# Naming the coming branch and its case ahead of each conditional weight split

## The chip, the cores and the metric

The kernel runs on one core of a Trainium2 chip. The metric is the device time of one execution in microseconds. The engines have short names in the profile: PE is TensorE (PEld its weight loads), DVE is VectorE, ACT is ScalarE, POOL is GpSimd, SP is SyncE, whose queue issues most of the DMAs. Each has a sequencer of its own, which takes the engine's instructions in order, handles registers, waits and branches by itself, and hands the rest to the engine.

## The reference

A retention layer without softmax (8 batches, 8 heads, 576 positions, head size 64), then two expert layers on its 4608 rows of 512. Each row goes to one of 8 experts, the one with the largest logit, and through that expert's two matrices with a relu between.

```python
scores = scale * np.matmul(q, k.transpose(0, 1, 3, 2))
ret = scores * Dmat[None, :, :, :]
x = np.matmul(ret, v)                 # then as rows [4608, 512]
...
expert_idx = np.argmax(logits, axis=1)
for e in range(E):
    mask = expert_idx == e
    h = np.maximum(x[mask] @ w1[e], 0.0)
    out[mask] = gate_w[mask, None] * (h @ w2[e])
```

The second expert layer does the same with its own gates and weights, and an output gate for each expert.

## The kernel before

Attention runs over 36 units of 128 tokens and scatters its rows by expert into a table in device memory, from which the first expert layer reads slots of 128 rows, all of one expert. It scatters its results into a second table for the second layer, which works alike and scatters to the output. Which expert a slot belongs to is known only at run time.

A product is made to about full precision from two parts of each operand: a high part rounded for fast TensorE passes and a low part, the difference. For the weights, `split_all` makes the parts from the raw buffers raw1 and raw2: ScalarE and VectorE copy the high parts (w1h, w2h, lines 298 and 299), VectorE and GpSimd subtract for the low ones (w1l, w2l, line 300). This is needed only at an expert's first slot, once for w1 and once for w2. So `switch(s, w)` (line 811) puts it into a two-way branch on ScalarE, VectorE and GpSimd: case 1 holds the split, case 0 holds nothing. `tc.Switch` gives each case a body that begins with a hint instruction naming the code behind the branch and ends with a jump there. The case is bit s of a mask that these engines hold in registers. After the branch SyncE refills the raw buffer for the next expert, if there is one to fetch.

The program gives every engine's order by hand. `period(t, n)` (line 1021) is one slot: TensorE makes slot t's first product (`first`, line 831), ScalarE and VectorE take its halves through the relu (`relu`, line 847), the next slot's rows are transposed and split (`trans_x`: xth on ScalarE, xtl on VectorE), then comes `switch(t + 1, 1)`, then the second product of slot t - 1 (`second`, line 865), the routing for the second layer (layer 1 only: route2a, route2b, chunk_logits with the copy lsb, and x1t), then `switch(t, 2)`, and `trans_h(t)` (line 855), in which ScalarE makes hth and VectorE htl for the second product of slot t. So each slot passes two branches, one for w1 of the next slot and one for w2 of its own. Layer 2 has `store` in place of the routing (oix on VectorE, line 889). The layers' last periods stand inside a further branch on the number of slots (line 1065).

In the profile the hint of a body has line 814, and the register and branch instructions of the dispatch have line 1259, the launch line.

Of the kernel before, what the change touches and what calls it, by code (L numbers as in the profile page):

```python
# [35 lines left out]

# columns of the constant table
C_ID = 0
# [23 lines left out]
def unit_table():  # L62
    """Units of 128 tokens: (batches, chunk); chunk 4 holds the tails of two batches."""
    u = []
    for bp in range(B // 2):
        for c in range(4):
            u.append(((2 * bp,), c))
            u.append(((2 * bp + 1,), c))
        u.append(((2 * bp, 2 * bp + 1), 4))
    return u  # L70
# [3 lines left out]
def retention_moe_moe(ctx, tc, qh, kth, kh, vh, embT, tau, w1, w2, wg, v1, v2, const, out):  # L74
# [51 lines left out]
    def inv_norm(pool, ss, n, tag, eng):  # L126
        """1 / (sqrt(ss) + 1e-6) by Newton steps on the reciprocal square root: tile and operations."""
        V = nc.vector
# [27 lines left out]
    def slot_tables(tab, cum_last, cum_part, psum):  # L156
        """From the counts, with slots along partitions: each slot's first row, which of its rows are
        its own, its expert's first slot, the next expert to fetch; and whether the first 256 rows of
        expert 0 were there by cum_part. TensorE's first step, the operations in order, and how many come
        before its second one (the last three serve the stores only); psum() gives a bank."""  # L160
        val, inv, ti, tf = tab
# [95 lines left out]
    def scatter_rows(key, table, rows, ix, n):  # L257
        """Rows to table[ix]; those past n are left out. No two scatters of a key share a row."""
        i = nc.gpsimd.indirect_dma_start(  # L259
            out=table,  # L260
            out_offset=bass.IndirectOffsetOnAxis(ap=ix, axis=0),
            in_=rows,
            in_offset=None,
            bounds_check=n - 1,
            oob_is_err=False,
        ).ins
        tc.declare_no_dep(i, group=key, reason="each row of the table is written by one scatter")
        tc.add_to_no_dep_group(key, i)
# [3 lines left out]
    def zero_heads(bk, i):  # L272
        """A third of the rows that a slot may read past those an expert has."""
        for r in ([e * NT for e in range(E)] + [P])[3 * i : 3 * i + 3]:
# [4 lines left out]
    def load_first(bk):  # L279
        """The first two tiles of expert 0's rows, ahead of the counts."""  # L280
        for i in range(2):
            nc.sync.dma_start(xs[i], bk[i * P : i * P + P, :])

    def split(i, r1, r2, w):
        """hi/lo parts of chunk i of w1 (w=1) or w2 (w=2): on which engine each half goes."""
        if w == 1:
# [7 lines left out]
    def split_ops(w, r1, r2):  # L294
        """The operations that split all of w1 or w2: hi(i) on ScalarE, sub(engine, i, columns) for lo, and
        for VectorE hi_v(i)."""
        ch = [split(i, r1, r2, w) for i in range(4)]
# [7 lines left out]
    def split_lists(w, r1, r2):  # L305
        """The same, shared out: for ScalarE, VectorE and GpSimd."""
        hi, hi_v, sub = split_ops(w, r1, r2)
# [10 lines left out]
    def load_raw(r1, r2, wa, wb, e, i=None):  # L318
        """Expert e's weights, whole or chunk i of 8 only."""
        for k in range(4):  # L320
# [7 lines left out]

    # ------------------------------------------------------------ attention
    ch = ExitStack()  # L330
    ch1 = ch.enter_context(tc.tile_pool(name="ch1", bufs=1, side="right"))
    ch2 = ch.enter_context(tc.tile_pool(name="ch2", bufs=2, side="right"))
    with ExitStack() as actx:
# [41 lines left out]

        # the tensor engine warms up while the first loads are under way
        nc.vector.memset(warm, 0.0)
# [107 lines left out]
        def cross(u):  # L485
            """The queries on the state before their unit."""
            bs, c = units[u]
# [117 lines left out]
        def pump(n):  # L605
            """Emit up to n queued small operations; one of TensorE opens a call or waits for the next."""
            first = True
# [155 lines left out]

    # ------------------------------------------------------------ experts
    mp = ctx.enter_context(tc.tile_pool(name="mp", bufs=1, reuse_waits="tile"))
# [10 lines left out]
    for t in orow:  # L776
        nc.gpsimd.memset(t[:, DM:ROW], 0.0)

    engs = {ET.DVE: nc.vector, ET.Pool: nc.gpsimd, ET.Activation: nc.scalar}
    everyone = {ET.PE: nc.tensor, ET.SP: nc.sync, **engs}  # L780
# [4 lines left out]
    def layer(which):  # L785
        """One expert layer's steps, by slot of 128 rows."""
        L = SimpleNamespace()
# [3 lines left out]
        ps_h, ps_o, rt, pk, sreg = {}, {}, {}, {}, {}  # L791
        L.state = (ps_h, ps_o, rt, pk, sreg)
        out_rows = (lambda s: orow[s % 4]) if g else (lambda s: yrow[s % 3])
# [17 lines left out]
        def switch(s, w):  # L811
            """At an expert's first slot: its weights from the raw buffer to their parts, the next one's there."""
            m, b = (L.mask[0], s) if s < NB else (L.mask[1], s - NB)
            for case in tc.Switch({e: (r >> b) & 1 for e, r in m.items()}, 2):  # L814
                if case == 1:
                    split_all(w, L.r1, L.r2)
            if w == 1:
                fetched(s)
            refill(w, *sreg[s])

        def fetched(s):
# [76 lines left out]
        def chunk_logits(s, copy=nc.scalar.copy):  # L898
            """Both gates' logits by chunk of 128 features, each chunk in its own 32 columns of the array."""
            rt[s] = pl = bank("M", f"pl{s}")  # L900
# [14 lines left out]
        def route2a(s):  # L915
            """Expert and place of each row of the second table: operations, the one-hots first."""
            V = nc.vector
# [56 lines left out]
        def redo():  # L974
            """Slots 0 and 1 again, now with the rows and the weights that the counts ask for."""
            masks()
# [15 lines left out]
        def begin(fail, late):  # L992
            """With the tables there: the loads that hang on them, slots 0 and 1 again if their rows were
            others, and the rest of these up to slot 0's second product."""
            for s in range(2, 5):
# [25 lines left out]
        def period(t, n):  # L1021
            """Slot t's first product, the one before's second, and what goes with them."""
            first(t)
# [3 lines left out]
            if t + 1 < n:  # L1027
                trans_x(t + 1)
                switch(t + 1, 1)
            second(t - 1, range(4))  # L1030
            if g and t >= 3:
# [50 lines left out]

    # attention's last tile goes to its expert while expert 0's first rows are at work
    psum = lambda: bank("C", "tabs")
# [30 lines left out]
    def turnover(n):  # L1115
        """The first layer's last slots to their experts while the second layer starts on expert 0."""
        for d in L2.state:
# [96 lines left out]
def _layout(inputs):  # L1214
# [4 lines left out]
    def units(a):  # L1219
        # [B, H, S, D] -> [units, 128 tokens, H, D]  # L1220
        a = a.transpose(0, 2, 1, 3)
# [41 lines left out]
```

## Time and profile before

| | us |
|---|---|
| median of 3 runs | 1527.78 |
| the three runs | 1527.77, 1527.78, 1530.72 |
| span of the profiled execution | 1519.3 |
| TensorE busy in that span | 1301.2 |
| VectorE busy | 634.8 |
| ScalarE busy | 420.0 |
| GpSimd busy | 369.6 |

The span runs from the first to the last instruction of the profiled execution; the time of a run also holds what lies before and behind it. Busy time counts operations on data alone. Registers, branches, waits and hints are the sequencer's and are not in it, and the timeline doesn't list them: their places are found by asking for their source line in a narrow stretch, which gives starts to a tenth of a microsecond.

### The profile page before, as it was taken

What the parts mean: (1) busy time and instruction counts of PE and PEld (TensorE: products, weight loads), DVE (VectorE), ACT (ScalarE), POOL (GpSimd) and SP (SyncE); (2) the same over time, 40 slices, a digit from 0 to 9 for tenths busy, and PEclk for the clock granted to TensorE, in tenths of its full rate; (3) what the DMA queues carried; (4) which work ended last, traced back from release to release, by engine and by line L of the source; (5) the groups of instructions that cost most, each with busy time, mean ns of one, the idle gap of its engine ahead of it and who ended that gap; (6) DMA issues with size and microseconds to landing.
All of it is one profiled execution on the core that took longest, in us unless ns stands there. A gap on an engine that the chain in (4) does not pass through costs nothing. (4 is left out here: it accounts for less than half of the span.)

```text
span 1519.3 us, 25914 instructions
## 1 busy us (share of the span) xinstructions
PE 1301.2 (86%) x7620; PEld 1051.6 (69%) x7620; DVE 634.8 (42%) x1589; ACT 420.0 (28%) x871; POOL 369.6 (24%) x431
## 2 busy tenths in 40 slices
PE   8899986888788887979788886898998789898988
PEld 7899975666566665757666674686776667676776
DVE  4566751443534444442544436124233442533331
ACT  2344431222222232322312222122232231322322
POOL 3477640220302121210212203003021221312121
PEclk9999998989899898989999998899998899999999
DMA  9999936233222214141231101413232433243110
GB/s 260 270 312 289 275 116 188 92 123 114 92 90 93 93 34 147 33 146 53 92 107 39 38 26 48 139 54 137 63 106 93 146 106 104 94 148 107 48 43 31
DMA packets 94255, 174.27 MB, mean 115 GB/s; under 512 B 8796, under 2 KB 36828, under 8 KB 92768
## 3 DMA queue, kind: packets, MB, share of 16 engines
q1 hardware_dynamic: 82144, 132.15, 28.8%
q0 software_dynamic: 9120, 28.91, 5.1%
q14 instruction: 1415, 11.59, 2.7%
q8 instruction: 72, 1.18, 0.3%
q10 hardware_dynamic: 1504, 0.43, 0.2%
HBM read 391.94 MB, written 35.36 MB: 281 GB/s over the span
## 5 line engine op out<-in xcount | busy, mean ns | idle before, releaser
L873 PE MATMUL po<-w2h,htl 128*128 128x512 f32 x624 | 270.8, 434 | 104.4 <-DVE htl L863 103.9
L873 PE MATMUL po<-w2h,hth 128*128 128x512 f32 x624 | 273.8, 439 | 23.3 <-ACT hth L862 21.7
L873 PE MATMUL po<-w2l,hth 128*128 128x512 f32 x624 | 262.4, 420 | 5.4 <-DVE w2l L300 5.4
L863 DVE TENSOR_TENSOR htl<-pt,hth 128x512 fp32r<-128x512 f32 x156 | 100.4, 684 | 381.5 <-issue 201.8
L873 PEld LDWEIGHTS po<-w2h,htl 128*128 128x128 f32 x624 | 129.1, 207 | 154.9 <-DVE htl L863 127.2
L838 PE MATMUL ph<-w1h,xth 128*128 128x512 f32 x624 | 206.4, 413 | 14.8 <-issue 10.9
L838 PE MATMUL ph<-w1l,xth 128*128 128x512 f32 x624 | 200.6, 403 | 9.3 <-DVE w1l L300 8.7
L838 PE MATMUL ph<-w1h,xtl 128*128 128x512 f32 x624 | 196.7, 397 | 0.0
L873 PEld LDWEIGHTS po<-w2h,hth 128*128 128x128 f32 x624 | 129.1, 207 | 56.1 <-ACT hth L862 23.6
L873 PEld LDWEIGHTS po<-w2l,hth 128*128 128x128 f32 x624 | 128.8, 206 | 33.0 <-DVE w2l L300 8.0
L862 ACT CAST hth<-pt 128x512 fp32r<-128x512 f32 x156 | 83.8, 588 | 244.6 <-issue 227.4
L838 PEld LDWEIGHTS ph<-w1l,xth 128*128 128x128 f32 x624 | 118.4, 193 | 45.0 <-DVE w1l L300 20.3
L259 POOL DMA_INDIRECT bk<-orow,bix x39 | 38.8, 996 | 444.5 <-DVE orow L967 288.1
L838 PEld LDWEIGHTS ph<-w1h,xtl 128*128 128x128 f32 x624 | 119.7, 192 | 26.9
L838 PEld LDWEIGHTS ph<-w1h,xth 128*128 128x128 f32 x624 | 113.9, 194 | 35.2 <-issue 16.1
L259 POOL DMA_INDIRECT out_dram<-yrow,oix x39 | 38.3, 982 | 389.8 <-ACTq L814 223.7
L300 POOL TENSOR_TENSOR w1l<-raw,w1h 128x1024 fp32r<-128x1024 f32 (+1 forms) x28 | 76.4, 2749 | 157.2 <-DVE w1h L299 157.2
L454 PE MATMUL sc<-qt,kt 128*128 128x128 f32 x576 | 83.6, 288 | 8.5 <-DMA kt<-in_kth_dram 7.6
L300 DVE TENSOR_TENSOR w1l<-raw,w1h 128x1024 fp32r<-128x1024 f32 (+1 forms) x42 | 87.4, 2133 | 0.0
L883 ACT ACTIVATE yrow<-po,xg 128x512 f32<-128x512 f32 x37 | 25.4, 688 | 211.9 <-PE po L873 169.6
L861 PE MATMUL pt<-ident,hs 128*128 128x128 f32 x624 | 83.2, 277 | 0.0
L300 DVE TENSOR_TENSOR w2l<-raw,w2h 128x1024 fp32r<-128x1024 f32 (+1 forms) x42 | 82.1, 2008 | 1.8 <-ACT w2h L298 1.8
(205 smaller groups left out, 1590.0 us busy)
## 6 DMA issues: line engine op xcount, KB each, us to landing
raw<-in_w_dram SPq DMA_DIRECT2D x77, 2048.0 KB
raw<-in_v_dram SPq DMA_DIRECT2D x77, 2048.0 KB
xg<-bk SPq DMA_DIRECT2D x74, 264.0 KB
qt<-in_qh_dram SPq DMA_DIRECT2D x36, 256.0 KB
vr<-in_vh_dram SPq DMA_DIRECT2D x36, 256.0 KB
kr<-in_kh_dram SPq DMA_DIRECT2D x36, 256.0 KB
kt<-in_kth_dram SPq DMA_DIRECT2D x70, 128.0 KB
bk<-z SPq DMA_DIRECT2D x18, 264.0 KB
```

What stands on the lines that cost most here:

```text
L259: i = nc.gpsimd.indirect_dma_start(out=table, out_offset=bass.IndirectOffsetOnAxis(ap=ix, axis=0), in_=rows, in_offset=None, bounds_check= ...
L300: sub = lambda eng, i, c=slice(0, FF): lambda: eng.tensor_sub(ch[i][1][:, c], ch[i][2][:, c], ch[i][0][:, c])
L454: nc.tensor.matmul(ps[:, j * P : j * P + P], k_t[:, hp, h, :], q_t[:, hp, :], start=(j == 0), stop=True, skip_group_check=True,)
L838: nc.tensor.matmul(ps_h[s][i], st[:, k, :], wt[:, i * 512 : i * 512 + 512], start=(k == 0 and wt is w1h[k] and st is xh), stop=(k == 3 or ...
L861: nc.tensor.transpose(ps[:, f, :], hsb[s % 2][:, o : o + P], ident)
L862: nc.scalar.copy(hth[s % 2][:, h, :], ps)
L863: nc.vector.tensor_sub(htl[s % 2][:, h, :], ps, hth[s % 2][:, h, :])
L873: nc.tensor.matmul(po, st[:, f, :], wt[:, b, :], start=(f == 0 and st is hh and wt is w2h[a]), stop=(f == 7 and st is hl),)
L883: nc.scalar.activation(o[:, 0:DM], ps_o.pop(s), AF.Copy, scale=x[:, DM : DM + 1])
```

## The change

`period` gets two calls of a new function `ahead(s, w)`. It asks for a hint instruction that names the branch of `switch(s, w)` and its case, worked out from the same mask bit, on the three engines that take the branch. The hint for w1 of the next slot stands at the start of a slot, ahead of its first product (from t = 3 on); the hint for w2 of the slot itself stands right behind the w1 branch and its refill. `switch` takes the label of the hint, so that hint and branch belong together. The bodies, the splits, the refills and all other operations are as before. (The diff also drops comments and docstrings, left out here.)

```diff
+        L.hints = {}
+        L.state = (ps_h, ps_o, rt, pk, sreg, L.hints)
...
         def switch(s, w):
-            m, b = (L.mask[0], s) if s < NB else (L.mask[1], s - NB)
-            for case in tc.Switch({e: (r >> b) & 1 for e, r in m.items()}, 2):
+            label = L.hints.pop((s, w), None)
+            for case in tc.Switch(at_first(s), 2, hint=label):
                 if case == 1:
                     split_all(w, L.r1, L.r2)
             if w == 1:
                 fetched(s)
             refill(w, *sreg[s])
+
+        def at_first(s):
+            m, b = (L.mask[0], s) if s < NB else (L.mask[1], s - NB)
+            return {e: (r >> b) & 1 for e, r in m.items()}
+
+        def ahead(s, w):
+            L.hints[s, w] = tc.switch_hint(at_first(s), 2, label=f"sw{which}_{s}_{w}_{next(uid)}")
...
         def period(t, n):
+            if t + 1 < n and t >= 3:
+                ahead(t + 1, 1)
             first(t)
             relu(t)
             if g:
                 trans_g(t - 2)
             if t + 1 < n:
                 trans_x(t + 1)
                 switch(t + 1, 1)
+                if t < n - 1:
+                    ahead(t, 2)
             second(t - 1, range(4))
```

## Rows read from the trace of the kernel before

**Rows 1.** In the page, its part on busy time: busy us, share of the span and instructions of each engine.
```profile
PE 1301.2 (86%) x7620; PEld 1051.6 (69%) x7620; DVE 634.8 (42%) x1589; ACT 420.0 (28%) x871; POOL 369.6 (24%) x431
```

**Rows 2.** The waits of the whole span. Columns: who waited at which line, for whom; us in total, times, longest us. "issue" is time in which the engine waited for nothing that the profile shows.
```profile
DVE htl L863 <- issue: 201.8, 33, 8.4
...
PE po L873 <- DVE htl L863: 103.9, 44, 5.5
...
DVE w2h L299 <- issue: 29.5, 9, 4.0
...
DVE w1h L299 <- issue: 28.4, 14, 3.3
...
PE pl L913 <- ACT lsb L910: 19.6, 13, 3.1
...
DVE w2h L299 <- PE px L827: 18.1, 5, 3.7
```

**Rows 3.** In the page, its part on DMA queues: the queue that carries instructions. Columns: packets, MB, share of 16 engines' time.
```profile
q14 instruction: 1415, 11.59, 2.7%
```

**Rows 4.** The instructions of line 814 over the whole span, those of the sequencers (DVEq is VectorE's). Columns: count, duration in ns (least, median, most), first and last start in us. The hint instruction stands first in each body of a branch.
```profile
L814 POOLq BRANCH_PREFETCH_HINT  x150: 31/38/43, 225.4 to 1498.9; - x150
L814 ACTq BRANCH_PREFETCH_HINT  x150: 31/31/36, 230.5 to 1505.0; - x150
L814 DVEq BRANCH_PREFETCH_HINT  x150: 39/44/45, 231.3 to 1505.6; - x150
```

**Rows 5.** The timeline of VectorE in a quiet slot of layer 1, 533 to 544 us. Columns: start us, us, engine, line, operation, tiles, shapes, count, and in brackets the idle time before it and what ended it.
```profile
533.73 0.17 DVE L962 SCALAR_TENSOR_TENSOR t<-pk,oh 128x8 f32<-128x8 f32 x1 [3.61 <-PE pt L861]
...
539.71 1.29 DVE L863 TENSOR_TENSOR htl<-pt,hth 128x512 fp32r<-128x512 f32 x2 [5.54 <-issue]
...
542.56 0.15 DVE L945 TENSOR_SCALAR W<-W 128x1 f32<-128x1 f32 x1 [0.16 <-ACT t L937]
542.63 0.68 DVE L853 TENSOR_SCALAR hs<-ph 128x512 f32<-128x512 f32 x1
```

**Rows 6.** The branch instructions of VectorE's sequencer in that slot (line 1259, where the program's own branches are recorded) and the hints that open the bodies (line 814), each answer for a narrow stretch. Columns as in rows 4.
```profile
L1259 DVEq COMPARE_BRANCH  x2: 52/64/75, 529.6 to 530.3; - x2
...
L1259 DVEq COMPARE_BRANCH  x1: 48/48/48, 534.4 to 534.4; - x1
...
L814 DVEq BRANCH_PREFETCH_HINT  x1: 44/44/44, 536.1 to 536.1; - x1
...
L1259 DVEq COMPARE_BRANCH  x1: 75/75/75, 536.3 to 536.3; - x1
...
L1259 DVEq MOVE  x2: 36/36/36, 543.6 to 543.7; - x2
...
L1259 DVEq COMPARE_BRANCH  x2: 52/64/75, 544.0 to 544.7; - x2
...
L814 DVEq BRANCH_PREFETCH_HINT  x1: 44/44/44, 544.5 to 544.5; - x1
```

**Rows 7.** The timeline of ScalarE in the same slot. Columns as in rows 5.
```profile
543.00 0.57 ACT L828 CAST xth<-px 128x512 fp32r<-128x512 f32 x1
```

**Rows 8.** The timeline of TensorE, in that slot and behind a split of w1 in layer 1. Columns as in rows 5.
```profile
543.96 0.17 PE L951 MATMUL pk<-oh,slb 128*128 128x8 bf16 x1 [0.73 <-DVE x1t L896]
...
653.05 0.79 PE L873 MATMUL po<-w2h,htl 128*128 128x512 f32 x1 [4.61 <-DVE htl L863]
```

**Rows 9.** The timeline of VectorE around a split of w1 in layer 1, 633 to 654 us. Columns as in rows 5.
```profile
633.01 0.15 DVE L945 TENSOR_SCALAR W<-W 128x1 f32<-128x1 f32 x1 [0.16 <-ACT t L937]
...
652.31 1.29 DVE L863 TENSOR_TENSOR htl<-pt,hth 128x512 fp32r<-128x512 f32 x2 [7.47 <-issue]
```

**Rows 10.** The last branch of VectorE ahead of that split and the hint in the split's body, and the same for a split of w2 in layer 1 (line 1259 and line 814 in narrow stretches). Columns as in rows 4.
```profile
L1259 DVEq COMPARE_BRANCH  x1: 48/48/48, 634.5 to 634.5; - x1
...
L814 DVEq BRANCH_PREFETCH_HINT  x1: 44/44/44, 637.5 to 637.5; - x1
...
L1259 DVEq COMPARE_BRANCH  x1: 52/52/52, 661.4 to 661.4; - x1
...
L814 DVEq BRANCH_PREFETCH_HINT  x1: 44/44/44, 664.2 to 664.2; - x1
```

**Rows 11.** The timeline of VectorE ahead of that split of w2: its first operation behind the way out of the branch before. Columns as in rows 5.
```profile
660.72 0.17 DVE L962 SCALAR_TENSOR_TENSOR t<-pk,oh 128x8 f32<-128x8 f32 x1 [3.61 <-issue]
```

**Rows 12.** The timeline of VectorE in layer 2, a quiet slot and the beginning of one with a split of w1. Columns as in rows 5.
```profile
1096.86 1.29 DVE L863 TENSOR_TENSOR htl<-pt,hth 128x512 fp32r<-128x512 f32 x2 [6.79 <-ACT hs L849]
...
1109.65 1.29 DVE L863 TENSOR_TENSOR htl<-pt,hth 128x512 fp32r<-128x512 f32 x2 [6.20 <-issue]
```

**Rows 13.** VectorE's branches and hints of those two (line 1259 and line 814 in narrow stretches). Columns as in rows 4.
```profile
L1259 DVEq COMPARE_BRANCH  x1: 48/48/48, 1097.6 to 1097.6; - x1
...
L814 DVEq BRANCH_PREFETCH_HINT  x1: 39/39/39, 1099.5 to 1099.5; - x1
...
L1259 DVEq COMPARE_BRANCH  x1: 48/48/48, 1110.7 to 1110.7; - x1
...
L814 DVEq BRANCH_PREFETCH_HINT  x1: 44/44/44, 1113.5 to 1113.5; - x1
```

**Rows 14.** ScalarE's sequencer in a split of w1 in layer 2: the hint in the body (line 814) and its first instruction behind the branch (line 883), in a narrow stretch. Columns as in rows 4.
```profile
L814 ACTq BRANCH_PREFETCH_HINT  x1: 31/31/31, 1025.2 to 1025.2; - x1
...
L883 ACTq EVENT_SEMAPHORE  x1: 38/38/38, 1027.3 to 1027.3; - x1
```

More of the change, by code (lines that the diff above doesn't have):

```diff
@@ L1 @@
+import itertools
 from contextlib import ExitStack
@@ L777, in retention_moe_moe @@
         nc.gpsimd.memset(t[:, DM:ROW], 0.0)
+    uid = itertools.count()
     engs = {ET.DVE: nc.vector, ET.Pool: nc.gpsimd, ET.Activation: nc.scalar}
@@ L791, in layer @@
         ps_h, ps_o, rt, pk, sreg = {}, {}, {}, {}, {}
-        L.state = (ps_h, ps_o, rt, pk, sreg)
+        L.hints = {}
+        L.state = (ps_h, ps_o, rt, pk, sreg, L.hints)
         out_rows = (lambda s: orow[s % 4]) if g else (lambda s: yrow[s % 3])
```

## The prediction

> **What bounds the kernel now.** I read first the busy shares, then the waits, then one quiet slot and one slot of each kind of split on VectorE, with the branch instructions of those slots.
>
> TensorE is busy 86% of the span, VectorE 42% [rows 1]. By shares alone TensorE is the bound. But the waits say that TensorE's largest idle time, 103.9 us in 44 pieces, is for htl, which VectorE writes, and that VectorE in its turn stood 201.8 us before htl with nothing to wait for that the profile shows [rows 2]. Such "issue" time is what a branch costs: the engine's next instructions are not there yet. Each of the three engines passes 150 of these branches [rows 4], and the queue that carries instructions moved 11.59 MB in 1415 packets [rows 3], some 8.2 KB each and some three packets for each of the 450 passes.
>
> In a quiet slot of layer 1 this can be timed. VectorE enters the empty body at 536.1, branches out some 0.2 us later, and its next operation, htl, starts at 539.71: the way out takes 3.4 us. The way in, from the branch at 534.4, takes 1.7 us; at the other branch, from 544.0 to 544.5, it takes 0.5 us [rows 5, 6]. Between the ways, VectorE works without a break (the one gap it has in 539.7 to 544.5 is 0.16 us). The slot therefore lasts as long as VectorE's loop, 14.4 us (the same branch stood at 529.6), and TensorE waits 0.73 us in it for x1t [rows 8]. So the resource that counts is VectorE's sequencer, and the four block fetches of a slot are more than half of it.
>
> Why does the way in differ? After a way out, the block behind the present one is on its way by itself: 533.7 (first operation after the way out) to 536.1 is 2.4 us, and by 544.5 it had long arrived, so that only 0.5 us was left [rows 5, 6]. The empty body lies in that next block, the split body one block further. A split body is thus entered late whatever came before: 634.5 to 637.5 is 3.0 us, 661.4 to 664.2 is 2.8 us [rows 10], and in layer 2 1110.7 to 1113.5 is 2.8 us [rows 13].
>
> **The change part by part.** It takes nothing away. It adds, per slot and engine, two groups of about six sequencer instructions. The branch itself is prepared by such a group, from its first MOVE at 543.6 to the branch at 544.0, and the hint instruction takes 0.04 us [rows 4, 6]: I price a hint at 0.45 us of VectorE's sequencer. ScalarE and GpSimd get the same.
>
> It can help only the way in, since the way out keeps the hint that already stands first in each body, and 3.4 us is what it costs with that hint. For an empty body it can help little: at 0.5 us there is nothing left, and where the way in takes 1.7 us the new hint stands right behind the way out, and names the block that is already coming.
>
> What is left are the splits: 14 of w1 and 14 of w2 (VectorE stood 28.4 us before the first operation of the one, 29.5 and 18.1 us before the other [rows 2]), half of them in each layer. The gain is not the 3 us of a way in but the lead that VectorE's program gives, because the hint is queued on the same engine behind its other work:
> - w1, layer 1. The hint can stand behind L945, at 633.01 [rows 9]; at 0.45 us it is out at 633.5. With the 3.0 us that the fetch took when it was asked for at the branch, the body is there at 636.5 instead of 637.5: 1.0 us, seven times, 7 us. The split, the way out behind it and htl at 652.31 [rows 9] move up by as much, and with htl TensorE, which waited 4.61 us for it [rows 8].
> - w1, layer 2. VectorE comes out at 1109.65, so the hint is out at 1110.2, and 3.0 us later is 1113.2 instead of 1113.5 [rows 12, 13]: 0.3 us, seven times, 2 us.
> - w2, both layers. VectorE comes out at 660.7 [rows 11], has only the few small operations of route2b, and branches at 661.4. The hint is out at 661.1 and the body there at 664.0 instead of 664.2: 0.2 us, fourteen times, 3 us. "Half a slot ahead" in the program is 0.3 us ahead here, as VectorE spent that half slot in the branch before.
>
> Together 12 us. Both ends: nothing, if the hint's block queues behind the one that comes by itself; and 28.4 + 29.5 + 18.1 = 76 us [rows 2] if every wait ahead of a split went.
>
> The costs. In a quiet slot of layer 1, the first group stands between L945 and the relu at 542.63. Relu and x1t start up to 0.45 us later, but the sequencer had to wait for xth in any case: the first MOVE of the branch is at 543.6, and ScalarE's xth ended at 543.57 [rows 6, 7]. So what counts is how far ScalarE's own group delays xth. The trace doesn't show it: 0 to 0.45 us, of which I take 0.2. Layer 1 has 150 / 2 / 2, some 37 such slots; without the seven of each split and the seven whose ways out are slowed by the refill (7.47 us before htl at 652.31 [rows 9]), 16 quiet ones are left: 3 us (0 to 7). The second group stands behind the way out, where the block of the next branch takes its 2.4 us regardless: nothing; if that cover went, 0.45 us a slot. In layer 2 the way in at 1097.6 ended at 1099.5, 2.6 us after htl's start at 1096.86 [rows 12, 13], so that both groups lie beside a fetch: nothing. On ScalarE the second group is ahead of lsb, for which TensorE waited 19.6 us in 13 pieces [rows 2]; some seven of them have ScalarE come straight out of a branch, at 0.4 us each: 3 us. GpSimd waits for others nearly always; its split operations come behind VectorE's first. Nothing moves on SyncE and no DMA of data is added.
>
> Sum: 12 - 3 - 3 = 6 us gained. The profiled execution has a span of 1519.3 us and the median is 1527.78, so 8.5 us lie around the span and don't change. **Forecast: 1522 us.** Its own range, from no gain with the costs to twice the gain, is 1510 to 1534.
>
> [...] In quiet slots a way in of 0.5 us shows that the next block had been fetched unasked [rows 6]. [...]
>
> **The rivals.**
> - A hinted block comes faster than one that is asked for at the branch. For: ScalarE entered a split body at 1025.2 with its hint, and had an instruction from behind the branch at 1027.3, 2.1 us later [rows 14]. Then the bodies above are there at 635.6, 1112.3 and 663.2: 1.9, 1.2 and 1.0 us, 13 + 8 + 14 = 36 us less 6 of costs: 1498. Against: there the hint names the very block that comes next anyway, and out of an empty body, where it does not, 3.4 us pass in spite of the hint [rows 5, 6].
> - Gain and cost cancel: the hinted block queues behind the one in flight, so that only the seven w1 splits of layer 1 gain, 7 us against 6: 1527. For: the 3.4 us again. Against: in layer 1 the next block has long landed when the w1 hint is given.
> - The hint fetches a block that is already there. In quiet slots of layer 1 the hint would be out at 543.1 and the body there 3.0 us later, at 546.1 instead of 544.5: 1.6 us in each of 16 slots, 26 us, and 1522 + 26 = 1548; the same follows if the hinted block pushes out the next one. It decides against the change from 0.4 us a slot on. Against: the 2.1 us of rows 14, where hint and next block were one and the fetch wasn't doubled, though it was still in flight then, not landed.
>
> **How the numbers follow.** Forecast 0.42; cancelled 0.26; faster blocks 0.14; fetched twice or pushed out 0.18. A measurement of this kernel can tell about 0.2%, 3 us, from no change. Of the forecast's share 0.32 lies below 1524.7, 0.07 within 3 us and 0.03 above; with 0.14 of the first rival, 0.23 and 0.03 of the second, and the third: faster 0.46, same 0.30, slower 0.24. The range that leaves out half of the first and of the third rival is 1498 to 1548.
>
> **What would show it.** The way in to the split of w1 in layer 1 should fall from 3.0 to about 2 us on VectorE, those to w2 hardly; ways out should stay at 3.4 us; VectorE's quiet slot should grow from 14.4 to 14.6 us in layer 1 and stay in layer 2; TensorE's waits for htl after a w1 split should shrink by 1 us. Empty bodies that are entered later than 0.5 us behind a long lead would show the third rival; split bodies entered after 1 us or less, everywhere, the first. I am wrong in the mechanism if the ways out change, as nothing here says that they should.

## The result, and the profile after

The changed kernel takes 1549.53 us in the median of four runs (1547.02 to 1550.63), against 1529.25 us for the kernel before in four runs beside it: a ratio of 1.0109, 95% interval 1.0079 to 1.0139. It is slower by 20 us where 6 us of gain were forecast. The profiled execution of it took 1547.02 us with a span of 1545.2 us. Ratios and their intervals, here and below, come from fast runs alone, so they can differ by a few tenths of a per cent from the quotient of two medians.

The page's part on busy time, its row of the queue that carries instructions, and two rows of the waits of the whole span (who waited, for whom: us, times, longest) answer to [rows 1 to 3]:
```profile
PE 1303.7 (84%) x7620; PEld 1055.7 (68%) x7620; DVE 640.4 (41%) x1589; ACT 423.5 (27%) x871; POOL 373.8 (24%) x431
```
```profile
q14 instruction: 1404, 11.50, 2.6%
```
```profile
PE po L884 <- DVE htl L874: 108.8, 45, 6.4
...
DVE w2h L300 <- issue: 42.0, 12, 4.4
```
The engines do the same work. TensorE waits 5 us longer for htl, and 8 us longer for w2l (13.8 us against 5.4). Ahead of w2's split VectorE stands as long as before: 42.0 us of "issue" and 6.5 us for TensorE, against 29.5 and 18.1 [rows 2]. The instruction queue moved 11 packets fewer, which says nothing of code fetched twice: two kernels without hints moved 1403 and 1416 (e13 and e14 below).

The next fence answers to [rows 10]: VectorE's sequencer at a split of w1 and at one of w2 in layer 1, each in a narrow stretch. Line 830 is the new hint, 1274 the branch, 817 the hint that is the first instruction in a body (columns: count, duration in ns, first and last start in us).
```profile
L830 DVEq BRANCH_PREFETCH_HINT  x1: 50/50/50, 570.9 to 570.9; - x1
...
L1274 DVEq COMPARE_BRANCH  x1: 59/59/59, 572.2 to 572.2; - x1
...
L817 DVEq BRANCH_PREFETCH_HINT  x1: 39/39/39, 575.1 to 575.1; - x1
...
L830 DVEq BRANCH_PREFETCH_HINT  x1: 50/50/50, 601.6 to 601.6; - x1
...
L1274 DVEq COMPARE_BRANCH  x1: 64/64/64, 602.4 to 602.4; - x1
...
L817 DVEq BRANCH_PREFETCH_HINT  x1: 39/39/39, 605.3 to 605.3; - x1
```
The ways in are 575.1 - 572.2 = 2.9 us and 605.3 - 602.4 = 2.9 us. Before, they were 3.0 and 2.8. The body was named 1.3 us and 0.8 us ahead of the branch and came no sooner.

What it costs stands in one quiet slot of layer 1: the instructions of line 830, and VectorE's operations around them in the timeline.
```profile
L830 DVEq MOVE  x3: 36/36/36, 540.7 to 541.1; - x3
L830 DVEq ALU_OP  x3: 45/50/58, 540.9 to 541.2; - x3
L830 DVEq FUSED_REGOPS  x1: 47/47/47, 541.0 to 541.0; - x1
L830 DVEq BRANCH_PREFETCH_HINT  x1: 50/50/50, 541.3 to 541.3; - x1
```
```profile
540.71 0.15 DVE L956 TENSOR_SCALAR W<-W 128x1 f32<-128x1 f32 x1 [0.16 <-ACT t L948]
541.37 0.69 DVE L864 TENSOR_SCALAR hs<-ph 128x512 f32<-128x512 f32 x1 [0.50 <-issue]
```
A hint is eight instructions, not the six that I had assumed, and with the instruction behind it 0.64 us pass (540.73 to 541.37), not 0.45. The timeline shows it as "issue" of 0.50 us ahead of relu, where [rows 5] have none.

To see which layer lost, take the first and last of VectorE's 38 relus in each layer: first the kernel before, then the changed one.
```profile
L853 DVE TENSOR_SCALAR hs<-ph x38: 678/681/693, 225.0 to 899.6; 128x512 f32<-128x512 f32 x38
...
L853 DVE TENSOR_SCALAR hs<-ph x38: 673/680/692, 947.8 to 1500.7; 128x512 f32<-128x512 f32 x38
```
```profile
L864 DVE TENSOR_SCALAR hs<-ph x38: 680/692/693, 225.8 to 914.6; 128x512 f32<-128x512 f32 x38
...
L864 DVE TENSOR_SCALAR hs<-ph x38: 675/681/694, 962.1 to 1526.9; 128x512 f32<-128x512 f32 x38
```
Layer 1 went from 674.6 to 688.8 us, layer 2 from 552.9 to 564.8: 14 + 12 us, the whole of the 26 us between the two profiled spans.

### The profile page after: what moved, and what is told of

The parts are those of the page before. It is cut to its first block, busy times and chain, and to the rows that moved or that the text cites. A ratio compares the mean times of both kernels' runs of the same rounds, so it can differ in the third digit from the quotient of the medians.

```text
span 1545.2 us, 29262 instructions
## 1 busy us (share of the span) xinstructions
PE 1303.7 (84%) x7620; PEld 1055.7 (68%) x7620; DVE 640.4 (41%) x1589; ACT 423.5 (27%) x871; POOL 373.8 (24%) x431
## 5 line engine op out<-in xcount | busy, mean ns | idle before, releaser
L884 PE MATMUL po<-w2h,htl 128*128 128x512 f32 x624 | 272.0, 436 | 109.1 <-DVE htl L874 108.8
L884 PE MATMUL po<-w2l,hth 128*128 128x512 f32 x624 | 263.4, 422 | 16.2 <-DVE w2l L301 13.8
```

The source lines that it names most:

```text
L884: nc.tensor.matmul(po, st[:, f, :], wt[:, b, :], start=(f == 0 and st is hh and wt is w2h[a]), stop=(f == 7 and st is hl),)
```

## The experiments

There were two questions. Why did the hints do nothing? "Dead": a hint of this form fetches nothing anywhere. "Late": a name counts only if it is given before the engine jumps into the group of instructions that ends in the named branch; once inside, only the code that follows in memory is fetched. "More lead": the hints stood too close to the branch. And what costs 20 us? "Instructions on VectorE", "others" (ScalarE and GpSimd), "wrong fetch", and later "place in memory".

**e1_early: the hints inside the bodies before.** Each conditional split's bodies, both of them, end in the hint for the next conditional split.
```
-            if t + 1 < n and t >= 3:
-                ahead(t + 1, 1)
-                if t < n - 1:
-                    ahead(t, 2)
 in switch(s, w, nxt):
             for case in tc.Switch(at_first(s), 2, hint=label):
                 if case == 1:
                     split_all(w, L.r1, L.r2)
+                if nxt:
+                    tc.switch_hint(at_first(nxt[0]), 2, label=L.hints[nxt])
```


> The hints are taken out of the groups and put at the end of both bodies of the conditional split before, so that each is given before the engine jumps back into the group that ends in the branch it names. Theory 'late' (a name counts only if it is given before the engine enters the stretch of code that holds the branch; inside that stretch only the code that follows in memory is fetched): VectorE's way into a split body falls from 2.8-3.1 us to about 0.5-1.3 us in the first layer, on ScalarE and GpSimd from 2.5 us to about 0.4-0.8 us, the 0.64 us of the hint is hidden in the empty body (whose way out shrinks by as much), and the time is below the kernel before by some 5 to 15 us: 1515 to 1525. Theory 'dead' (the hint in this form fetches nothing wherever it stands): ways into a split body stay at 2.8-3.1 us on VectorE and 2.5 us on the others, and the time is that of the kernel before or up to 10 us above it: 1528 to 1540.

Measured: 1501.33 us, ratio 0.9791 (0.9761 to 0.9820). VectorE's sequencer at a split of w1 and one of w2 in layer 1 (823 is the hint, 1270 the branch, 819 the body's first instruction), then ScalarE's at the first of them:
```profile
L823 DVEq BRANCH_PREFETCH_HINT  x1: 45/45/45, 544.8 to 544.8; - x1
...
L1270 DVEq COMPARE_BRANCH  x1: 56/56/56, 553.1 to 553.1; - x1
...
L819 DVEq BRANCH_PREFETCH_HINT  x1: 44/44/44, 553.7 to 553.7; - x1
...
L823 DVEq BRANCH_PREFETCH_HINT  x1: 45/45/45, 574.8 to 574.8; - x1
...
L1270 DVEq COMPARE_BRANCH  x1: 56/56/56, 578.6 to 578.6; - x1
...
L819 DVEq BRANCH_PREFETCH_HINT  x1: 44/44/44, 580.4 to 580.4; - x1
```
```profile
L1270 ACTq COMPARE_BRANCH  x1: 37/37/37, 551.7 to 551.7; - x1
...
L819 ACTq BRANCH_PREFETCH_HINT  x1: 31/31/31, 552.1 to 552.1; - x1
```
The ways in fall from 2.9 us to 0.6 and 1.8, on ScalarE to 0.4. "Dead" is out. The gain, 28 us, is nearly twice the upper end of what I expected. The ways in of ScalarE and GpSimd fell as well; which engine brought how much isn't shown.

**e2_early_other: the same, naming the wrong body.**
```
-                    tc.switch_hint(at_first(nxt[0]), 2, label=L.hints[nxt])
+                    tc.switch_hint({e: 1 - v for e, v in at_first(nxt[0]).items()}, 2, label=L.hints[nxt])
```


> As e1_early, but each hint names the other body, the one that will not be entered. Theory 'late': the ways into an empty body on VectorE rise from 0.5 us to 2.5-3 us in the first layer, on ScalarE and GpSimd from 0.4 us likewise, split bodies stay at 2.8 us, and a quiet slot of two empty bodies is some 4 us longer: 1600 us or more. Theory 'dead': the same as e1_early within 5 us, and no way in changes.

Measured: 1654.75 us, ratio 1.0829 (1.0792 to 1.0865). VectorE at an empty body of layer 1, where the way in was 0.5 us in [rows 6]:
```profile
L1270 DVEq COMPARE_BRANCH  x1: 56/56/56, 569.5 to 569.5; - x1
...
L819 DVEq BRANCH_PREFETCH_HINT  x1: 44/44/44, 572.1 to 572.1; - x1
```
It is 2.6 us now: with the other body named in that place, the one that follows in memory came 2.1 us later. With the right one named, that one came early (0.6 us in e1).

**e3_swap: the kernel before with its bodies in the other order.**
```
-            for case in tc.Switch({e: (r >> b) & 1 for e, r in m.items()}, 2):
-                if case == 1:
+            for case in tc.Switch({e: 1 - ((r >> b) & 1) for e, r in m.items()}, 2):
+                if case == 0:
                     split_all(w, L.r1, L.r2)
```


> The kernel before, without hints, with the two bodies in the other order: the split is case 0 and so directly behind the branch, the empty body is case 1. Theory that the code that follows in memory is fetched by itself (whoever says this of the hints): VectorE's way into a split body in the first layer falls from 2.8-3.0 us to 0.5-1.3, its way out rises from 0.5 us to 2.6-3.4; the way into an empty body rises from 0.5-1.6 us to 2.8 and its way out falls from 3.4 to about 2.6 us or below. A quiet slot becomes longer by 2 x (2.3 - 0.8) = 3 us: 1560 to 1590 us. If the ways hang on what a body holds and not on where it lies: nothing moves, 1527 to 1532.

Measured: 1579.99 us, ratio 1.0319 (1.0288 to 1.0349). VectorE at a split of w1 and at an empty body, layer 1, no hint ahead of either:
```profile
L1259 DVEq COMPARE_BRANCH  x1: 52/52/52, 578.2 to 578.2; - x1
...
L814 DVEq BRANCH_PREFETCH_HINT  x1: 39/39/39, 578.7 to 578.7; - x1
...
L1259 DVEq COMPARE_BRANCH  x1: 52/52/52, 561.9 to 561.9; - x1
...
L814 DVEq BRANCH_PREFETCH_HINT  x1: 39/39/39, 564.8 to 564.8; - x1
```
The split is now entered after 0.5 us and the empty body after 2.9. (The splits of w2 in this layer, whose branch stands closer behind a way out, are entered after 1.5 to 1.8 us.) In both orders the body that lies next behind the branch came early without being named: the empty one after 0.5 us in [rows 6], the split after 0.5 us here.

**e9_behind_jump: as early as the group allows.** The hint is the first thing behind the jump out of the body before.
```
                 switch(t + 1, 1)
+                if t < n - 1:
+                    ahead(t, 2)
...
                 switch(t, 2)
+                if t != T_FIX - 1:
+                    ahead(*((t + 2, 1) if t + 2 < n else (t + 1, 2)))
```


> The hints of the changed kernel moved as far forward as they go without being inside a body: each stands directly behind the conditional split before the one it names, so it is the first thing VectorE, ScalarE and GpSimd do after the jump back into the group. The lead over its branch is then almost that of e1_early (5 us and more in a quiet slot), only the side of the jump differs. Theory 'late' (only a name given before that jump counts): ways into a split body stay at 2.8-3.1 us on VectorE in the first layer and at 2.5 us on ScalarE and GpSimd, and the time is at or above that of the changed kernel: 1540 to 1560 us. Theory 'more lead' (e1_early won because its hints came some 5 us sooner): the ways in fall to 0.5-1.9 us as they did there, and the time is below the kernel before, 1500 to 1525 us.

Measured: 1565.56 us, ratio 1.0196 (1.0157 to 1.0234). VectorE at a split of w1 in layer 1:
```profile
L830 DVEq BRANCH_PREFETCH_HINT  x1: 50/50/50, 571.9 to 571.9; - x1
...
L1274 DVEq COMPARE_BRANCH  x1: 64/64/64, 576.3 to 576.3; - x1
...
L817 DVEq BRANCH_PREFETCH_HINT  x1: 39/39/39, 579.1 to 579.1; - x1
```
With a lead of 4.4 us, longer than the way in itself, the way in is 2.8 us. In e1 a lead of 3.8 us (574.8 to 578.6), given on the other side of the jump, brought 1.8. "More lead" is out, and "late" is left: the side of the jump decides. The time is worse than that of the changed kernel. One of the two hints now stands ahead of htl, and TensorE waits 128.1 us for htl in place of 108.8; that this is the reason was not tested by itself.

**e11_long_empty: does the hint at the head of a body work?** It names the body's own end, and stands in the body.
```
                 if case == 1:
                     split_all(w, L.r1, L.r2)
+                else:
+                    for q in engs.values():
+                        for i in range(4):
+                            vload(q, TI_TOT, E - 1)
```


> The kernel before with four loads of a register from a table in each empty body, so that the body lasts 2 us or more between the hint at its head, which names its end, and the jump out of it. It is far slower, and its time is not the question. If the hint at the head of a body starts a fetch at once, the way out of an empty body (3.4 us on VectorE, 2.9 us on ScalarE and GpSimd) falls towards 0.5-1 us. If that hint too comes after the fetch of the next code in memory has been begun, and so does nothing, the way out stays at 2.6 us or more.

Measured: 1714.72 us in a single run. VectorE in an empty body of layer 1, and its first instruction behind it:
```profile
L814 DVEq BRANCH_PREFETCH_HINT  x1: 39/39/39, 566.9 to 566.9; - x1
...
L1263 DVEq COMPARE_BRANCH  x1: 75/75/75, 569.7 to 569.7; - x1
...
L966 DVEq EVENT_SEMAPHORE  x1: 21/21/21, 572.5 to 572.5; - x1
```
The end is named 2.8 us before the jump, and the way out still takes 2.8 us. So a hint at the head of a body, as all bodies had it all along, brought no short way out even with that lead.

**e5 to e8 and e12: where the cost lies.** Hints on one side only; the arithmetic alone; every hint twice; hints for w1 only.
```
 e5   tc.switch_hint({ET.DVE: at_first(s)[ET.DVE]}, ...)
 e6   tc.switch_hint({e: v for e, v in at_first(s).items() if e != ET.DVE}, ...)
 e7   v = {e: ((x << 1) + 1) >> 1 for e, x in v.items()}   (twice)
      L.hints[s, w] = {e: engs[e].snap(x & 1) for e, x in v.items()}
      ... for case in tc.Switch(L.hints.pop((s, w), None) or at_first(s), 2):
 e8   for _ in range(2):
          tc.switch_hint(at_first(s), 2, label=label)
 e12  -                if t < n - 1:
      -                    ahead(t, 2)
```


> The changed kernel with its hints on VectorE alone. Theory 'instructions on VectorE' (the hint fetches nothing where it stands; its eight instructions, 0.64 us each time, lengthen VectorE's serial loop): nearly the whole loss stays, 1543 to 1551 us, with VectorE's quiet slot at about 14.7 us. Theory 'others' (the loss comes over ScalarE's late xth, lsb and hth copies): most of the loss goes, 1528 to 1536 us.

> The changed kernel with its hints on ScalarE and GpSimd alone. Theory 'instructions on VectorE': little of the loss is left, 1528 to 1536 us. Theory 'others': the loss stays, 1543 to 1551 us.

> The changed kernel with the naming instruction taken out: at each place of a hint the three engines do register arithmetic of about as many instructions (the case number, seven more operations that leave it as it is, a copy), and the branch later uses that copy. Theory 'instructions on VectorE': the same time as the changed kernel within 5 us, 1543 to 1553. Theory 'wrong fetch' (the hint starts or delays a fetch, and that costs): the loss goes, 1527 to 1535 us.

> The changed kernel with every hint given twice. Theory 'instructions on VectorE': the loss about doubles, as another 0.5 to 0.6 us is added 142 times: 1565 to 1580 us. Theory 'wrong fetch': a second hint that names the same body moves nothing, and costs only its own issue where VectorE has time to spare: 1547 to 1557 us.

> The changed kernel with only the hint ahead of the split of w1 in each slot, not the one ahead of w2. As the forecast had it, the w1 hints would carry most of the gain (9 of 12 us). Theory 'instructions on VectorE': half of the instructions and up to half of the loss, 1533 to 1542 us, and w1 ways in unchanged at 2.8-3.1 us. Theory 'wrong fetch': the loss sits where most split bodies are entered late, so nearly all of it or none: 1545 to 1550 us or 1528 to 1532.

Measured, as ratios to the kernel before:

| run | us | ratio | interval |
|---|---|---|---|
| e5, VectorE only | 1548.18 | 1.0098 | 1.0075 to 1.0122 |
| e6, ScalarE and GpSimd only | 1541.13 | 1.0055 | 1.0028 to 1.0082 |
| e7, arithmetic only | 1541.35 | 1.0046 | 1.0027 to 1.0065 |
| e8, twice | 1602.70 | 1.0446 | 1.0418 to 1.0474 |
| e12, w1 only | 1533.21 | 1.0022 | 0.9999 to 1.0046 |

VectorE's hints alone cost nearly the whole, but those of the others alone cost half of it, so the two don't add up. Twice the hints cost four times as much, and half of them no more than the noise. No theory had e6 and e8 together. In the profiled executions, layer 1, from its first relu to its last, lasts 682.5 us in e5, 692.1 in e6, 713.9 in e8 and 673.9 in e12, against 674.6 before and 688.8 with all hints: there the hints of ScalarE and GpSimd alone lose most, and the w1 hints alone nothing. A loss that grows faster than the hints would fit added time that is hidden at first, beside a fetch or a wait; e17 asks for that. In e7 the compiler put the arithmetic directly ahead of the branch, so it didn't ask what it was meant to.

**e10 and e17: the arithmetic, held in its place.** A move into a fixed register keeps it where the hint stood. In e10 that register is the case number; in e17 it is the mask, so that the branch does all its own work.
```
 e10  x = three times ((x << 1) + 1) >> 1 of the case number
      engs[e].reg_mov(named[e], x)
 e17  for _ in range(5):
          x = ((x << 1) + 1) >> 1                     (x: the mask)
      engs[e].reg_mov(named[e], x)
      the branch: (named >> b) & 1
```


> As e7, whose arithmetic the compiler put directly ahead of the branch; here a move into a fixed register holds it at the place of the hint. No hint is given. Theory 'instructions on VectorE': with 0.5 to 0.7 us of register operations at the place of each hint the loss of the changed kernel comes back, 1543 to 1555 us. Theory 'wrong fetch': the time is that of the kernel before to e7, 1529 to 1541 us.

> No hint; register operations of about 0.6 us at the place of each hint, as in e10, but the branch now does the same work as in the changed kernel (0.38 us on VectorE, against 0.24 us in e10). Theory 'instructions on VectorE': the first layer's stretch is that of the changed kernel within 3 us (688 to 689), and the time is 1540 to 1553 us, the second layer hanging on the place of the code. Theory 'naming costs by itself': the first layer's stretch is that of the kernel before (673 to 675), and the time 1525 to 1540 us.

Measured: e10 1524.54 us, ratio 0.9959 (0.9940 to 0.9978); e17 1531.16 us, ratio 1.0012 (0.9991 to 1.0034). In e17, the added instructions on VectorE over the whole span, the operation behind them in a quiet slot, and the relus of layer 1:
```profile
L834 DVEq FUSED_REGOPS  x372: 182/196/237, 261.2 to 1451.5; - x186
```
```profile
547.69 0.69 DVE L869 TENSOR_SCALAR hs<-ph 128x512 f32<-128x512 f32 x1 [0.56 <-issue]
```
```profile
L869 DVE TENSOR_SCALAR hs<-ph x38: 681/692/693, 227.0 to 897.2; 128x512 f32<-128x512 f32 x38
```
Relu is held up by 0.56 us of "issue" here, by 0.50 in the changed kernel: the time added on VectorE is the same. Yet layer 1 lasts 670.2 us, not 688.8. My theory of VectorE's instructions falls: their time alone doesn't bring the loss. What e17 does not have is the naming instruction, and it has three longer instructions where a hint has eight.

Where the loss lies can be read from VectorE's ways into empty bodies. The branch of w2 behind one and the same split of w1 in layer 1, first in the changed kernel (lines 1274 and 817), then in e17 (lines 1279 and 817):
```profile
L1274 DVEq COMPARE_BRANCH  x1: 64/64/64, 395.9 to 395.9; - x1
...
L817 DVEq BRANCH_PREFETCH_HINT  x1: 45/45/45, 400.8 to 400.8; - x1
...
L1279 DVEq COMPARE_BRANCH  x1: 48/48/48, 393.4 to 393.4; - x1
...
L817 DVEq BRANCH_PREFETCH_HINT  x1: 39/39/39, 393.9 to 393.9; - x1
```
The way in takes 4.9 us with hints and 0.5 without. Seven empty bodies of layer 1 are entered like this in the changed kernel, after 2.4 to 4.9 us (branches at 331.5, 395.9, 464.1, 531.5, 595.1, 701.0 and 764.3); e17 enters the same seven after 0.5 to 0.9 us. (One more, at 358.8 us, is late in every kernel.) Over 29 slots, 273.8 to 818.1 us here and 272.2 to 802.5 us in e17, the changed kernel is 14.0 us longer, and the seven slots with these entries hold 13.7 of them. The kernel before has three late entries (305.9, 438.7 and 693.8, after 2.2 to 2.5 us). It loses some 4 us by them against e17, and e17 loses as much over its other slots, some 0.16 us each, so the added time is not quite free.

**e13 to e16: the place of the code in memory.** Register loads at the start of attention, twelve or twenty-four, move all code behind them, in the kernel before (e13, e14) and in the changed one (e15, e16).
```
+        zt = cp.tile([1, 1], I32, name="zt")
+        nc.vector.memset(zt, 0)
+        for q in (nc.vector, nc.scalar, nc.gpsimd):
+            for _ in range(12):
+                q.value_load(zt[0:1, 0:1], min_val=0, max_val=1)
```


> The kernel before with twelve loads of a register from a table on VectorE, ScalarE and GpSimd once, at the start of attention: 36 more instructions ahead of all the rest, some 8 us of an engine that has little to do there, up to 8 us on the time. Theory 'place in memory': the stretch from the first to the last relu of each layer, 674.5 and 553.0 us in the kernel before, moves by several us up or down in one layer or both, as other groups now cross the end of a stretch of code. Theory 'instructions on VectorE': both stretches stay within 2 us.

> As e13 with twenty-four loads, 72 instructions. Theory 'place in memory': the two layers' stretches differ again from those of the kernel before and of e13 by several us. Theory 'instructions on VectorE': they stay within 2 us of 674.5 and 553.0.

> The changed kernel with the same twelve loads as e13. Theory 'instructions on VectorE': it is slower than e13 by what the changed kernel is slower than the one before, 14 to 22 us. Theory 'place in memory': the difference is another one, anywhere from -5 to 35 us, and the slots that are 2.8 to 3.6 us longer in the changed kernel (three in the first layer, each with a way into an empty body of 2.4 us and more) are others or none.

> The changed kernel with the twenty-four loads of e14. Theory 'instructions on VectorE': 14 to 22 us above e14. Theory 'place in memory': another difference than that of e15 to e13 and of the changed kernel to the one before.

Measured: 1531.57, 1544.79, 1552.82 and 1562.16 us; ratios 0.9994 (0.9978 to 1.0011), 1.0085 (1.0057 to 1.0113), 1.0136 (1.0107 to 1.0165) and 1.0188 (1.0157 to 1.0218). VectorE's relus of layer 1 in e13, e14, e15, e16:
```profile
L858 DVE TENSOR_SCALAR hs<-ph x38: 679/681/692, 222.2 to 896.3; 128x512 f32<-128x512 f32 x38
```
```profile
L858 DVE TENSOR_SCALAR hs<-ph x38: 679/681/690, 232.7 to 905.8; 128x512 f32<-128x512 f32 x38
```
```profile
L869 DVE TENSOR_SCALAR hs<-ph x38: 678/691/693, 223.7 to 913.1; 128x512 f32<-128x512 f32 x38
```
```profile
L869 DVE TENSOR_SCALAR hs<-ph x38: 681/691/693, 233.7 to 921.8; 128x512 f32<-128x512 f32 x38
```
Layer 1 lasts 674.1 and 673.1 us without hints, 689.4 and 688.1 with them: a loss of 15 us wherever the code lies. Over the same 29 slots it lies again in those with a late entry: five of them hold 12.8 of the 13.2 us that e15 is longer than e17, and five 10.9 of 11.8 us in e16. Layer 2 in e13 and in e14:
```profile
L858 DVE TENSOR_SCALAR hs<-ph x38: 673/680/691, 943.4 to 1507.5; 128x512 f32<-128x512 f32 x38
```
```profile
L858 DVE TENSOR_SCALAR hs<-ph x38: 673/680/692, 952.8 to 1521.4; 128x512 f32<-128x512 f32 x38
```
The changed kernel is 21 us and 17 us slower than its partner, as it was 20 us slower unmoved. "Place in memory" falls as the cause of the loss. The second layer scatters: 564.1 and 568.6 us here and 571.1 in e17, without hints, as much as in the changed kernel, but 553.1 in e6, with some. Of the 12 us that I read there from one execution of each kernel, some 8 go with a quick execution of the kernel before, whose span is that much below its median run's.

**e4_inline and e18_inline_shift24: no bodies at all.** The split stands in the stream, behind a compare and skip on all five engines; e18 adds the loads of e14.
```
-            for case in tc.Switch({e: (r >> b) & 1 for e, r in m.items()}, 2):
-                if case == 1:
-                    split_all(w, L.r1, L.r2)
+            with tc.If((m >> b) & 1):
+                split_all(w, L.r1, L.r2)
...
-            L.mask = [{e: vload(q, TI_MASK + i, (1 << NB) - 1) for e, q in engs.items()} for i in range(2)]
+            L.mask = [nc.values_load(ti[0:1, TI_MASK + i : TI_MASK + i + 1], min_val=0, max_val=(1 << NB) - 1) for i in range(2)]
```


> The kernel before, without hints, with each conditional split as a plain compare-and-skip on all five engines in place of the two aligned bodies. If the price of a slot is the fetch of bodies and not the hint: packets of the instruction queues fall by more than half from 1415, VectorE's ways in and out (0.5 + 3.4 us twice a slot) vanish, its loop falls from 14.4 us to about 7 us and TensorE sets a slot of about 13.7 us: 1440 to 1500 us. If a skipped split costs a fetch anyway: 1520 to 1560 us.

> e4 with the twenty-four loads of e14 and e16 on the three engines at the start. If the place of the code counts only where there are bodies to fetch, the time is that of e4 (1281) plus what the loads cost at the start (up to 10 us in e14): 1281 to 1291 us, and the layers' stretches stay at 511.5 and 477.9 us within 2 us.

Measured: e4 1280.83 us, ratio 0.8369 (0.8349 to 0.8389); e18 1288.98 us, ratio 0.8424 (0.8397 to 0.8451). Of e4, busy time, the instruction queue, TensorE's wait for htl, its first product behind the chunk of po in two slots that follow each other, and VectorE's relus:
```profile
PE 1220.8 (96%) x7620; PEld 1020.6 (80%) x7620; DVE 650.7 (51%) x1589; ACT 425.7 (33%) x871; POOL 355.7 (28%) x431
```
```profile
q14 instruction: 125, 1.02, 0.3%
```
```profile
PE po L872 <- DVE htl L862: 12.9, 7, 1.8
```
```profile
503.38 0.17 PE L950 MATMUL pk<-oh,slb 128*128 128x8 bf16 x1 [0.94 <-DVE x1t L895]
...
516.87 0.18 PE L950 MATMUL pk<-oh,slb 128*128 128x8 bf16 x1
```
```profile
L852 DVE TENSOR_SCALAR hs<-ph x38: 680/691/692, 224.6 to 736.0; 128x512 f32<-128x512 f32 x38
...
L852 DVE TENSOR_SCALAR hs<-ph x38: 673/692/692, 781.7 to 1259.6; 128x512 f32<-128x512 f32 x38
```
The queue moves 125 packets in place of 1415, TensorE waits 12.9 us for htl in place of 103.9 [rows 2] and is busy 96% of the span. A quiet slot takes 13.5 us (503.38 to 516.87) in place of 14.4. The layers take 511.4 and 477.9 us: 163 and 75 us less. I had expected 1440 to 1500, by quiet slots; but 0.9 us in some 16 of these is only 14 of the 163 us, and the rest lies in the other slots. The first layer of e18, on the same rows, lasts 512.0 us: here the place of the code costs nothing, and the 8 us more are the loads at the start. TensorE's part in e4 is not waiting alone: of the 241 us by which the span is shorter, 161 are its idle time and 80 its busy time, for the same 7620 products at a mean granted clock of 0.985 in place of 0.935.

## Why the prediction was wrong

**The step that failed** is the gain: "at 0.45 us it is out at 633.5. With the 3.0 us that the fetch took when it was asked for at the branch, the body is there at 636.5 instead of 637.5". It took for granted that a fetch begins when the hint is executed. The runs show no sign of that while the engine was already in the group that ends in the branch: the ways into split bodies of layer 1 stayed at 2.8 to 3.1 us with a lead of 0.8 and 1.3 us, and at 2.8 us with one of 4.4 us (e9). What came after 0.5 us without a hint was the body next in memory (e3). (The last slots of a layer have some shorter ways into split bodies, with hints and without: 0.9 to 1.4 us in the changed kernel, from 1.8 us on in the one before; they were not followed up.) All 12 us of gain were therefore 0. I had "nothing, if the hint's block queues behind the one that comes by itself" as the lower end, and the row that bore on it was before me: a way out of 3.4 us in spite of a hint [rows 5, 6]. I took it for what a way out costs, and didn't ask why the hint in the body brought nothing.

**The costs** were 3 + 3 us, and 20 were measured. The terms of that sum were not far off. The hint takes 0.64 us and not 0.45, but the second group does hide beside the fetch (the way in behind it takes 1.0 us in place of 1.7, from 547.9 to 548.9), TensorE's wait for lsb grew from 19.6 to 21.5 us, and in e17 time of this length costs some 0.16 us a slot. What the sum put at nothing is the way into the empty bodies, which it left at 0.5 and 1.7 us: seven late entries hold 13.7 of the 14.0 us by which the 29 slots of layer 1 are longer than in e17. "In layer 2 nothing" is not far off once e13 and e14 are the measure: with hints the layer is 5 and 3 us longer there (e15 and e16), within its scatter.

**What stays open** is why empty bodies are entered late more often with the hints. The same seven are late with hints on VectorE alone (e5) and with the hints behind the jump (e9); with the w1 hints alone (e12) and with e17's register operations none of these is. So neither the added time nor the naming of w1's bodies brings them. The amount of code in a slot is a candidate, and so are the w2 hints. A run that gives eight instructions without a name would tell them apart; it wasn't made. And e6, in which VectorE enters its bodies as in the kernel before, loses 18 us of layer 1 in another way, which was not followed.

**The rivals.** "Gain and cost cancel" had the cause nearly right (the body next in memory comes first, after 0.5 us against 2.9 in e3) and still counted 7 us of gain. "Fetched again or pushed out" gave 1548, next to the 1549.53 measured. Its sign came, empty bodies that are entered late, but in seven slots of layer 1 and not in 16, and kernels without hints have such entries too; so the close number is in part luck, and whether a hint pushes anything out there is open. For hints given before the jump, e2 shows the next body coming later when the other is named, after 2.6 us in place of 0.5. "Faster blocks" is out.

**The blocks of code** that the prediction counts with, a next one and one further on, were my estimate: no run shows where one ends. What the runs show is the order of the bodies, 0.5 us into the one next in memory and 2.9 us into the other (e3), and that a body which is not the next is entered after 0.6 us when it is named before the jump (e1). Without bodies the kernel is 249 us of 1530 shorter (e4).

**Right were** that ways out would stay (3.1 and 3.5 us in the quiet slot at 542.5 us, 3.3 and 3.4 before), that the supply of instructions bounds the kernel (e4, 1280.83 us, which took the bodies from all three engines, so that VectorE's share in it is not shown), and that a split body is late because of where it lies (e3: put first, it is entered after 0.5 us in place of 3.0 [rows 10]). A quiet slot takes 14.7 us (542.5 to 557.2), next to the 14.6 that I had forecast. **Wrong in passing** was the 8.5 us around the span: the changed kernel's profiled execution of 1547.02 us has a span of 1545.2, so 2 us lie around it, and the rest was one execution's distance from the median. So were two small sums, by about 1 us each: 1109.65 + 0.45 is 1110.1 and not 1110.2, and with 3.0 us the body of w2 would be there at 664.1 and not at 664.0.

## What to carry over

- A hint's lead counted here by where it stood, not in microseconds: put it in front of the jump into the code that ends in the branch, here in the bodies of the branch before (a lead of 3.8 us there brought a way in of 1.8 us in e1, one of 4.4 us behind the jump 2.8 us in e9), and check one way in against one without a hint.
- Before you hide the fetch of a branch's body, ask whether it needs a body of its own: skipping a rare piece of work in the stream removed the fetches (1415 to 125 packets) and 16% of the time, the hints at their best 2%.
- A difference in one stage between two single profiles is worth little until kernels that should agree have been laid beside it: layer 2 scattered by 18 us between four kernels without hints.
- Where a loss doesn't fit the average slot, list every pass in order: seven bad ones held nearly all of it here.

## What the runs showed of the hardware, unexpected

- With no hint ahead of the branch, the way into the body next in memory took 0.5 us, or 1.7 us close behind a way out [rows 6], and into the body behind it 2.8 to 3.0 us [rows 10], or 2.9 us with the two in the other order (e3).
- A hint given before the jump shortened VectorE's ways into split bodies from 2.9 us to 0.6 and 1.8 (e1; ScalarE's took 0.4), and one that named the wrong body lengthened the way into an empty one from 0.5 to 2.6 us (e2). Behind the jump, with 4.4 us of lead, the way in was 2.8 us (e9), and behind a hint at the head of a body, with 2.8 us, the way out 2.8 us (e11).
- Register arithmetic, 0.56 us of it in a quiet slot, cost 0.1%, which is within noise (e17), hints of 0.64 us at 142 places 1.1%, those of w1 alone 0.2%, which is within noise as well (e12), and hints given twice 4.5% (e8).
